# Linear attention followed by a gated MLP: in half of the batches the keys' sums become the stationary operand of the product with q

## The chip, the cores and the metric

The kernel runs on one core of a Trainium2 chip. Its engines work side by side: TensorE (PE in the profile; PEld is its loading of weights, the stationary operand), VectorE (DVE), ScalarE (ACT), GpSimd (POOL), and SyncE (SP), whose queue issues all DMAs here. PSUM is the memory that matmuls write; SBUF is where their operands lie. The metric is the device time of one execution in microseconds (us), as the median of several executions.

## What is computed

```python
# q, k, v: (8 batches, 8 heads, 576 positions, 64); omega: (128, 64); float32
def phi(x):                                   # x is scaled by 64 ** -0.25
    h = x @ omega.T - sum(x * x) / 2
    return exp(h - max(h)) / sqrt(128)        # 128 features of a position
q_p, k_p = phi(q), phi(k)
kv  = einsum('bhsm,bhsd->bhmd', k_p, v)       # 128 x 64 for a head
z   = sum(k_p, axis=2)                        # 128 for a head
num = einsum('bhsm,bhmd->bhsd', q_p, kv)
den = einsum('bhsm,bhm->bhs', q_p, z) + 1e-6
x   = (num / den) as 4608 rows of 512         # 8 heads x 64
out = (silu(x @ w_gate) * (x @ w_val)) @ w_out   # 512 -> 1536 -> 512
```

The MLP's weights come as 64-bit floats and are turned into 32-bit ones on the chip.

## The kernel before

**Groups and steps.** The attention is cut into groups of 256 positions of one pair of heads (`kgroups` and `qgroups`, L101 to L103). 576 positions give two such groups and 64 left over, and the left-over 64 positions of all four pairs make one more group, the one whose `gr` is None. So a batch has 9 groups of k and 9 of q. A step (L110 to L113) handles two groups: in steps 0 to 5 two of k, then 60 times one of q and one of k that lies 12 groups ahead, and in the last 6 steps two of q. A group of q goes through stages that are steps apart: projection and exponential (`st_transpose`, `st_project`, `st_max`, `st_exp`) in its own step, `q_transpose` one step later, `q_mult` two and `q_out` three steps later (L69 to L71).

**A group of q.** `st_exp` leaves the features `ph`: 128 positions on the partitions, 2 chunks by 2 heads by 128 features. `q_transpose` (L473) turns them by four PE transposes into `ptq` in PSUM, and ACT copies that to `qt`: 128 features on the partitions, 2 heads by 256 positions. `q_mult` (L486) has `qt` stationary: per chunk and head a matmul with 128 positions as columns of the weights, and `kvst`, 64 columns of kv and one of z, streams through. `po` then holds positions on the partitions, with the numerator in 64 columns and the denominator in the 65th. DVE adds the epsilon, inverts, and multiplies (L504 to L512) into `xn`. `q_out` (L520) turns `xn` by two transposes into `xt`, whose partitions are the 2 x 64 values of the two heads; ACT rounds it into `xh` and DVE takes the rest as `xl`, the MLP's x in two parts.

In the left-over group the four pairs have 64 positions each, so the weights are 64 columns wide, and two pairs use the two column halves of the array.

**The keys.** `k_accumulate` (L440) sums kv and z of two pairs in one PSUM tile `kvacc`, and `kv_finalize` (L433) copies it by ACT to `kvr` when all groups have been added, twice in a batch. z is the 65th column of `kvr`: a column of 128 features for each head.

**PSUM.** The tiles made by `ps_att` (L87) share one buffer of one bank: `pt` (the transposed inputs), `ptq`, `po` and `xt` follow one another in it. `pp`, `kvacc` and the MLP have buffers of their own.

**The MLP.** `stream` (L600) goes over ten tiles of up to 512 rows in rounds of two or three tiles, and over four sets of three weight slices in each round. A product is made of three matmuls of rounded parts: high by high, high by low, low by high. ACT makes the high part of a weight (`whi`, L237) and POOL the low part (`wlo`, L238); of the hidden layer, ACT makes `hh` (L641) and POOL `hl` (L642). `acc` collects a tile's rows over the sets, in buffers of the pool `accp`, which `om2` uses too.

**Order.** `ORDER` (L671) lists the nine stages of a step; after each of them `give` hands out a share of the step's MLP matmuls, so that attention and MLP are interleaved by a course that is worked out beforehand (L177 to L192). The framework may move an instruction ahead of one whose operands it reckons to be late; each engine then runs its own list strictly in order. Behind the loop the rest of the MLP runs alone.

Of the kernel before, what the change touches and what calls it, by code (L numbers as in the profile page):

```python
# [11 lines left out]
F32 = mybir.dt.float32  # L12
# [4 lines left out]
ALU = mybir.AluOpType  # L17
AX = mybir.AxisListType
# [5 lines left out]
def kernel(  # L24
# [11 lines left out]
    nc = tc.nc  # L36
    B, H, S, D = q.shape
    M = omega.shape[0]
    NT, DM = out.shape
    DF = w_gate.shape[1]  # L40
    P = 128
    NPAIR = H // 2
# [3 lines left out]
    NF = DF // P  # L46
    G = 256
    CH = G // P
# [6 lines left out]
    EPS = 1e-6 * M  # L55
    RES = S % G
# [8 lines left out]
    LAV = 1  # L65
    KLAG = 2
    TLAG = 1
    MLAG = 2
    OLAG = 3  # L69


    const = ctx.enter_context(tc.tile_pool(name="const", bufs=1))
    xres = ctx.enter_context(tc.tile_pool(name="xres", bufs=NXB))
    wpool = ctx.enter_context(tc.tile_pool(name="wpool", bufs=FA))
    moe = ctx.enter_context(tc.tile_pool(name="moe", bufs=2))
    accp = ctx.enter_context(tc.tile_pool(name="accp", bufs=11))
    dram = ctx.enter_context(tc.tile_pool(name="dram", bufs=1, space=DRAM))
    ps_m = ctx.enter_context(tc.tile_pool(name="ps_m", bufs=4, space=PSUM))
    att = ctx.enter_context(tc.tile_pool(name="att", bufs=2))
# [4 lines left out]
    ident = const.tile([P, P], F32, name="ident")  # L84
    make_identity(nc, ident)

    def ps_att(name, shape):  # L87
        return ps_a.tile(shape, F32, name=name, tag="b")
# [27 lines left out]
    def slots(n, kind):  # L116

        if not 0 <= n < NS:
            return []
        return [(i, b, g, (kgroups if kd == "k" else qgroups)[g]) for i, (kd, b, g) in enumerate(steps[n]) if kd == kind]  # L120

    def pairs_of(gr):
        return [(2 * c, 2 * c + 1) for c in range(CH)] if gr is None else [gr[:1]] * CH
# [3 lines left out]
    def column(b, gr):  # L127
        return b * S + (S - RES if gr is None else gr[1])
# [10 lines left out]
    def tile_of(col):  # L139
        j = max(j for j, (c, _) in enumerate(TILES) if c <= col)  # L140
        return j, col - TILES[j][0]
# [27 lines left out]
    for n in range(NS):  # L169
        for i, b, g, gr in slots(n, "q"):  # L170
            first = column(b, gr)
            for j in {tile_of(first)[0], tile_of(first + (RES if gr is None else G) - 1)[0]}:
                whole[j] = n + OLAG
                begun.setdefault(j, n + OLAG)


    NN = NS + OLAG + 1  # L177
    upper, lower = np.zeros(NN + 1), np.zeros(NN + 1)
# [48 lines left out]
    weights = {}  # L227
    converted = set()
# [48 lines left out]
    def tick():  # L277
        ticks[0] += 1
        next(wa, None)
# [74 lines left out]
    box = {}  # L354
# [3 lines left out]
    def st_transpose(n):  # L358
        if n >= NS:
            return  # L360
        nat = nats.pop(n)
        pt = (ps_moe if n < DENSE else ps_att)(f"pt_{n}", [P, 2, G])
        for i in range(2):
            for c in range(CH):
                nc.tensor.transpose(  # L365
                    pt[:, i, c * P : (c + 1) * P], nat[:, i, c].rearrange("p h d -> p (h d)"), ident
                )
        x = att.tile([P, 2, G], F32, name=f"x_{n}", tag="x")

        st = att.tile([P, 4, 2, CH, 2], F32, name=f"st_{n}", tag="st", bufs=6)  # L370
        sq = att.tile([P, 2, CH, 2, D], F32, name=f"sq_{n}", tag="sq")
        nc.gpsimd.tensor_tensor(sq, nat, nat, op=ALU.mult)  # L372
        nc.scalar.copy(x, pt)
        sts[n] = x, st, sq
        return True
# [51 lines left out]
    kvst = {}  # L427
# [5 lines left out]
    def kv_finalize(b, a2):  # L433
        acc = kvacc.pop((b, a2))
        raw = att.tile([P, 4, VW], F32, name=f"kvr{b}_{a2}", tag="kvr", bufs=4)
        nc.scalar.copy(raw, acc)
        for j in range(2):
            kvst[b, 2 * a2 + j] = raw[:, 2 * j : 2 * j + 2, :]

    def k_accumulate(n, half):  # L440

# [28 lines left out]
    qts = {}  # L470
    xns = {}

    def q_transpose(n):  # L473
        m = n
        n -= TLAG
        for _, b, g, gr in slots(n, "q"):
            ph = box.pop(("q", b, g))
            pt = (ps_moe if m < EARLY else ps_att)(f"ptq{b}_{g}", [P, 2, G])
            for hh in range(2):
                for c in range(CH):  # L480
                    nc.tensor.transpose(pt[:, hh, c * P : (c + 1) * P], ph[:, c, hh * M : (hh + 1) * M], ident)  # L481
            qts[b, g] = att.tile([P, 2, G], F32, name=f"qt{b}_{g}", tag="qt")
            nc.scalar.copy(qts[b, g], pt)
        return bool(slots(n, "q"))

    def q_mult(n):  # L486

        n -= MLAG
        for _, b, g, gr in slots(n, "q"):
            qt = qts.pop((b, g))  # L490
            po = ps_att(f"po{b}_{g}", [P, CH, 2, VW])
            for c in range(CH):
                prs = pairs_of(gr)[c]
                w = P // len(prs) if gr is None else P
                for j, pr in enumerate(prs if gr is None else prs[:1]):
                    for hh in range(2):
                        nc.tensor.matmul(  # L497
                            po[j * w : (j + 1) * w, c, hh, :],
                            qt[:, hh, c * P + j * w : c * P + (j + 1) * w],
                            kvst[b, pr][:, hh, :],  # L500
                            start=True, stop=True, skip_group_check=True,
                        )
            dn = att.tile([P, 2, CH, 2], F32, name=f"dn{b}_{g}", tag="dn", bufs=4)
            nc.vector.tensor_scalar_add(dn[:, 0], po[:, :, :, D], EPS)  # L504
            nc.vector.reciprocal(dn[:, 1], dn[:, 0])
            xn = att.tile([P, CH, 2, D], F32, name=f"xn{b}_{g}", tag="xn", bufs=3)
            nc.vector.tensor_tensor(
                xn.rearrange("p c h d -> p (c h) d"),
                po[:, :, :, 0:D].rearrange("p c h d -> p (c h) d"),
                dn[:, 1].rearrange("p c (h o) -> p (c h) o", o=1).broadcast_to([P, 2 * CH, D]),  # L510
                op=ALU.mult,
            )  # L512
            xns[b, g] = xn
        return bool(slots(n, "q"))
# [5 lines left out]
    def q_out(n):  # L520
        n -= OLAG
        for _, b, g, gr in slots(n, "q"):
            xn = xns.pop((b, g))
            po = ps_att(f"xt{b}_{g}", [P, G])
            first = column(b, gr)
            for c in range(CH):
                nc.tensor.transpose(po[:, c * P : (c + 1) * P], xn[:, c].rearrange("p h d -> p (h d)"), ident)  # L527
            j, o = tile_of(first)
            if gr is None:
                parts_ = [(po.rearrange("d (r c) -> d r c", c=RES), slice(0, NPAIR), j, o, RES)]  # L530
            else:
                cut = min(TILES[j][1] - o, G)
                parts_ = [(po[:, 0:cut], gr[0], j, o, cut)]
                if cut < G:
                    parts_.append((po[:, cut:G], gr[0], j + 1, 0, G - cut))
            for src, pr, j, o, w in parts_:
                if j not in xt:

                    while j - NXB >= 0 and not finished(j - NXB):
                        assert give(1), "the MLP waits for x, and x for the MLP"  # L540
                    xt[j] = [xres.tile([P, NPAIR, T], F32R, name=f"x{e}{j}", tag=f"x{e}") for e in "hl"]
                hi, lo = (t[:, pr, o : o + w] for t in xt[j])
                nc.scalar.copy(hi, src)
                nc.vector.tensor_tensor(lo, src, hi.bitcast(F32), op=ALU.subtract)  # L544
            if gr is None or gr[0] == NPAIR - 1:
                cols_done[0] = first + (RES if gr is None else G)
        return bool(slots(n, "q"))
# [23 lines left out]
    def finished(j):  # L571

        return at_visit[0] > last_visit[j]
# [83 lines left out]
    def give(us):  # L657
        debt[0] += us
        while debt[0] > 0:
            u = next(ma, None)  # L660
            if u is None:
                debt[0] = 0.0
                return False
            debt[0] -= u
            given[0] += u
        return True
# [3 lines left out]

    ORDER = (  # L671
        st_project,
        q_out,
        lambda n: st_transpose(n + 1),
        q_mult,
        lambda n: k_accumulate(n, 0),
        st_max,
        q_transpose,
        lambda n: k_accumulate(n, 1),
        st_exp,  # L680
    )

    for n in range(2):
# [7 lines left out]
    for n in range(NN):  # L691
        load(n + LA)
        load_v(n + LAV)
        want = OPS * np.interp(clock[n + 1], [clock[m] for m, _ in marks], [x for _, x in marks])
        for i, what in enumerate(ORDER):
            left = len(ORDER) - i
            what(n)
            due = course[n + 1] - given[0] - debt[0]
            if due > 0:
                give(due / left)  # L700
            for _ in range(int(np.ceil((want - ticks[0]) / left))):
                tick()
    for _ in ma:
        pass

# [29 lines left out]
```

## Time and profile before

| | |
|---|---|
| median of 3 runs | 1291.54 us (1289.42 to 1296.39) |
| profiled execution | 1285.57 us |
| its span, first to last instruction | 1283.8 us |
| granted TensorE clock, mean | 0.982 |
| matmul instructions | 7329 |
| DMA | 95.71 MB, 74 GB/s of HBM traffic over the span |

The span lies 1.8 us inside the time of its execution. Busy times of PE overlap: a matmul's duration in the profile is the time from its start until its result is out, and the next one starts long before. What a matmul costs is read from the distance between starts. A float32 matmul appears as two instructions (two passes), an fp32r matmul and a transpose as one.

### The profile page before, as it was taken

To read this page: it belongs to the slowest core of one execution; us is meant where nothing else is said; L and a number is where in the kernel's file an instruction comes from. 1 tells how busy PE (TensorE), PEld (TensorE's weight loads), DVE (VectorE), ACT (ScalarE), POOL (GpSimd) and SP (SyncE) were. 2 spreads that over 40 slices of the span, in tenths; PEclk is the share of its full clock that TensorE was granted. 3 is DMA by queue.
4 is the path that set the end of the run, shared out by engine and by line. 5 is a ranking of instruction groups with operands and counts; after the bars stand their busy time and mean duration, and the time that the engine had idled before them with its cause. 6 is when DMAs were issued, how large, how long until landed. Compare 5 with 4: busy or idle time off the path is not lost.

```text
span 1283.8 us, 19309 instructions
## 1 busy us (share of the span) xinstructions
PE 1243.3 (97%) x7329; PEld 1039.1 (81%) x7329; DVE 514.2 (40%) x1080; ACT 629.0 (49%) x1358; POOL 419.1 (33%) x364
## 2 busy tenths in 40 slices
PE   6988999999989999999999999999999999999998
PEld 5977778887868888888878888888888878888887
DVE  4787774457742343223333333223333321121212
ACT  4865666565344554555556653854544323222211
POOL 3454241545444121333333311433322113242421
PEclk7997899999989999999999999999999999999999
DMA  6557552345432122221222221211110111111112
GB/s 161 137 159 192 141 160 63 86 136 154 125 95 62 42 67 63 60 64 50 65 59 50 65 51 41 66 50 50 51 41 26 34 33 34 41 43 32 50 27 57
DMA packets 156477, 95.71 MB, mean 75 GB/s; under 512 B 119520, under 2 KB 131808, under 8 KB 156384
## 3 DMA queue, kind: packets, MB, share of 16 engines
q1 hardware_dynamic: 156384, 94.47, 28.0%
q8 instruction: 58, 0.95, 0.3%
q14 instruction: 35, 0.29, 0.1%
HBM read 75.56 MB, written 18.87 MB: 74 GB/s over the span
## 4 chain that ended last, share of the span: by engine, by line
PE 81%; DVE 7%; ACT 3%; issue 3%; POOL 2%; DMA 2%; SPq 1%; POOLq 0%; ACTq 0%; DVEq 0%
PE o L567 21%; PE g L558 21%; PE v L558 19%; PE pp L388 6%; PE kvacc L458 5%; PE po L497 4%; PE ptq L481 2%; PE pt L365 2%; ACT ph L420 1%; PE xt L527 1%; DVE st L261 1%; DVE st L406 1%; POOL wlo L238 1%; DMA nat<-in_k_dram 1%; SPq L323 1%
## 5 line engine op out<-in xcount | busy, mean ns | idle before, releaser
L642 POOL TENSOR_TENSOR hl<-sl,hh 128x512 fp32r<-128x512 f32 (+1 forms) x120 | 145.0, 1208 | 288.9 <-ACT hh L641 285.6
L238 POOL TENSOR_TENSOR wlo<-wraw,whi 128x512 fp32r<-128x512 f32 x108 | 138.9, 1299 | 251.7 <-ACT whi L237 230.0
L420 ACT ACTIVATE ph<-pp,st 128x128 f32<-128x128 f32 x576 | 166.6, 388 | 55.1 <-DVE st L409 54.0
L558 PE MATMUL g<-xh,whi 128*128 128x512 f32 (+1 forms) x480 | 184.4, 387 | 0.5 <-DVE sl L638 0.4
L558 PE MATMUL v<-xh,whi 128*128 128x512 f32 (+1 forms) x480 | 184.0, 383 | 0.0
L567 PE MATMUL o<-whi,hh 128*128 128x512 f32 x432 | 178.1, 412 | 2.4 <-ACT whi L237 1.7
L558 PE MATMUL g<-xl,whi 128*128 128x512 f32 (+1 forms) x480 | 180.0, 375 | 0.0
L558 PE MATMUL g<-xh,wlo 128*128 128x512 f32 (+1 forms) x480 | 178.8, 372 | 0.0
L558 PE MATMUL v<-xh,wlo 128*128 128x512 f32 (+1 forms) x480 | 178.1, 371 | 0.0
L558 PE MATMUL v<-xl,whi 128*128 128x512 f32 (+1 forms) x480 | 177.6, 370 | 0.0
L567 PE MATMUL o<-wlo,hh 128*128 128x512 f32 x432 | 171.5, 397 | 2.0 <-DVE st L408 1.4
L567 PE MATMUL o<-whi,hl 128*128 128x512 f32 x432 | 171.2, 396 | 0.3 <-POOL hl L642 0.2
L641 ACT CAST hh<-sl 128x512 fp32r<-128x512 f32 (+1 forms) x120 | 69.9, 584 | 172.7 <-DVE sl L638 172.3
L638 DVE TENSOR_TENSOR sl<-v,sl 128x512 f32<-128x512 f32 (+1 forms) x120 | 76.3, 636 | 188.0 <-PE v L558 181.9
L372 POOL TENSOR_TENSOR sq<-nat 128x512 f32<-128x512 f32 x72 | 77.4, 1076 | 213.0 <-DMA nat<-in_k_dram 192.8
L591 DVE TENSOR_TENSOR acc<-o,acc 128x512 f32<-128x512 f32 x108 | 74.3, 690 | 178.4 <-PE o L567 177.9
L406 DVE TENSOR_REDUCE st<-pp 128x4 f32<-128x512 f32 x144 | 93.5, 684 | 103.0 <-PE pp L388 103.0
L237 ACT CAST whi<-wraw 128x512 fp32r<-128x512 f32 x108 | 66.9, 623 | 103.9 <-PE v L558 58.5
L558 PEld LDWEIGHTS g<-xh,wlo 128*128 128x128 f32 x480 | 91.3, 190 | 15.2
L558 PEld LDWEIGHTS g<-xh,whi 128*128 128x128 f32 x480 | 91.2, 191 | 15.3 <-DVE sl L638 0.6
L558 PEld LDWEIGHTS v<-xh,wlo 128*128 128x128 f32 x480 | 90.4, 188 | 15.3
L558 PEld LDWEIGHTS g<-xl,whi 128*128 128x128 f32 x480 | 91.6, 191 | 13.2 <-DVE xl L544 0.3
(56 smaller groups left out, 1872.1 us busy)
## 6 DMA issues: line engine op xcount, KB each, us to landing
wraw<-wscr SPq DMA_DIRECT2D x108, 256.0 KB, 2.8
wscr<-wc SPq DMA_DIRECT2D x36, 256.0 KB, 2.2
out_dram<-acc SPq DMA_DIRECT2D x72, 128.0 KB, 2.3
nat<-in_k_dram SPq DMA_DIRECT2D x64, 128.0 KB, 3.1
v<-in_v_dram SPq DMA_DIRECT2D x64, 128.0 KB, 3.1
nat<-in_q_dram SPq DMA_DIRECT2D x64, 128.0 KB, 2.7
st<-in_moe_w_gate_dram SPq DMA_DIRECT2D x12, 512.0 KB, 4.4
st<-in_moe_w_val_dram SPq DMA_DIRECT2D x12, 512.0 KB, 4.6
```

The lines of the kernel that those rows point to most:

```text
L237: nc.scalar.copy(hi, raw)
L238: nc.gpsimd.tensor_tensor(lo, raw, hi.bitcast(F32), op=ALU.subtract)
L372: nc.gpsimd.tensor_tensor(sq, nat, nat, op=ALU.mult)
L388: nc.tensor.matmul(pp[hh][:, i, c, :], x[r, i, c * P : (c + 1) * P], omT[r], start=True, stop=True)
L406: nc.vector.tensor_reduce(st[:, 1, :, :, hh], pp[hh], axis=AX.X, op=ALU.max, negate=True)
L420: nc.scalar.activation(ph[:, c, hh * M : (hh + 1) * M], pp[hh][:, i, c, :], AF.Exp, bias=st[:, 3, i, c, hh : hh + 1], scale=1.0,)
L558: nc.tensor.matmul(ps, a_[:, ws], b_[:, c, :], start=n == 0, stop=n == 3 * NC - 1)
L567: nc.tensor.matmul(ps, a_[:, ts_], b_, start=first and n == 0, stop=last and n == 2)
L591: nc.vector.tensor_tensor(a_, po, a_, op=ALU.add)
L638: nc.vector.tensor_tensor(h, pv, h, op=ALU.mult)
L641: nc.scalar.copy(hh, h)
L642: nc.gpsimd.tensor_tensor(hl, h, hh.bitcast(F32), op=ALU.subtract)
```

## The change

For the batches 4 to 7 (`BPOOL = 4`, counted from 0) the product with q is turned round, and the division by the denominator is done ahead of it.

- `kv_finalize` also transposes the z columns of the two pairs (128 x 4) on PE into `zp` (4 x 128, in the shared PSUM buffer), copies them by ACT, and writes these 2 KB to DRAM.
- `load_z`, at the end of the step that has a batch's first group of q, reads them back with each row spread over all 128 partitions: two DMAs into `zt`, in a buffer of the raw weights that is no longer needed.
- `q_den`, a new last stage, one step behind the exponential: POOL multiplies `ph` by z (128 x 512; four instructions in the left-over group), DVE sums over the features, adds the epsilon and inverts.
- `q_norm`, a new second stage, two steps behind: POOL multiplies `ph` in place by these factors.
- `q_transpose` comes two steps behind the exponential in place of one, on the scaled `ph`.
- `q_mult` does nothing for these batches.
- `q_out` computes `xt` directly: for each head one matmul with 64 columns of `kvst` stationary and 256 columns of `qt` streaming, written to the head's half of the partitions (four pairs by 64 columns in the left-over group).

The pool `accp` has 10 buffers in place of 11, and `xn` shares two buffers with POOL's product, in place of three of its own. The batches 0 to 3 keep the old form.

```diff
-    accp = ctx.enter_context(tc.tile_pool(name="accp", bufs=11))
+    accp = ctx.enter_context(tc.tile_pool(name="accp", bufs=10))
...
+        if b >= BPOOL:
+            zp = ps_att(f"zp{b}_{a2}", [4, P])
+            nc.tensor.transpose(zp, raw[:, :, D], ident)
+            zs = att.tile([4, P], F32, name=f"zs{b}_{a2}", tag="zs")
+            nc.scalar.copy(zs, zp)
+            zd = dram.tile([4, P], F32, name=f"zd{b}_{a2}", tag="zd", bufs=4)
+            nc.sync.dma_start(zd, zs)
+            zds[b, a2] = zd
...
+    def load_z(n):
+        for _, b, g, gr in slots(n, "q"):
+            if g == 0 and b >= BPOOL:
...
+                zt = att.tile([P, 2, 4, M], F32, name=f"zt{b}", tag="stw")
+                for a2 in range(2):
+                    nc.sync.dma_start(
+                        zt[:, a2], zds.pop((b, a2)).rearrange("(o h) m -> o h m", o=1).broadcast_to([P, 4, M])
+                    )
+                    zbc[b, a2] = zt[:, a2]
...
+    def q_den(n):
+        n -= JLAG
...
+                nc.gpsimd.tensor_tensor(
+                    jk, ph, zt.rearrange("p (o h) m -> p o h m", o=1).broadcast_to([P, CH, 2, M]), op=ALU.mult
+                )
+            dn = att.tile([P, 3, CH, 2], F32, name=f"dj{b}_{g}", tag="dj", bufs=6)
+            nc.vector.tensor_reduce(dn[:, 0], jk, axis=AX.X, op=ALU.add)
+            nc.vector.tensor_scalar_add(dn[:, 1], dn[:, 0], EPS)
+            nc.vector.reciprocal(dn[:, 2], dn[:, 1])
+            dns[b, g] = dn
+
+    def q_norm(n):
+        n -= NLAG
...
+            nc.gpsimd.tensor_tensor(
+                phv, phv,
+                dn[:, 2].rearrange("p c (h o) -> p (c h) o", o=1).broadcast_to([P, 2 * CH, M]),
+                op=ALU.mult,
+            )
...
     def q_transpose(n):
         m = n
-        n -= TLAG
-        for _, b, g, gr in slots(n, "q"):
+        todo = [(b, g) for _, b, g, gr in slots(n - TLAG, "q") if b < BPOOL]
+        todo += [(b, g) for _, b, g, gr in slots(n - NLAG, "q") if b >= BPOOL]
+        for b, g in todo:
...
     def q_mult(n):
...
+            if b >= BPOOL:
+                continue
...
     def q_out(n):
...
+            if b < BPOOL:
+                xn = xns.pop((b, g))
+                for c in range(CH):
+                    nc.tensor.transpose(po[:, c * P : (c + 1) * P], xn[:, c].rearrange("p h d -> p (h d)"), ident)
+            else:
+                qt = qts.pop((b, g))
+                segs = [(pr, pr * RES, RES) for pr in range(NPAIR)] if gr is None else [(gr[0], 0, G)]
+                for pr, o, w in segs:
+                    for hh in range(2):
+                        nc.tensor.matmul(
+                            po[hh * D : (hh + 1) * D, o : o + w], kvst[b, pr][:, hh, 0:D], qt[:, hh, o : o + w],
+                            start=True, stop=True, skip_group_check=True,
+                        )
...
     ORDER = (
         st_project,
+        q_norm,
         q_out,
...
         st_exp,
+        q_den,
     )
```

More of the change, by code (lines that the diff above doesn't have):

```diff
@@ L67 @@
     TLAG = 1
+    JLAG = 1
+    NLAG = 2
     MLAG = 2
     OLAG = 3
+    BPOOL = 4
     const = ctx.enter_context(tc.tile_pool(name="const", bufs=1))
@@ L438, in kv_finalize @@
             kvst[b, 2 * a2 + j] = raw[:, 2 * j : 2 * j + 2, :]
+        if b >= BPOOL:
[6 more added lines that the diff above has]
+            zds[b, a2] = zd
+    zds = {}
+    zbc = {}
+    def load_z(n):
+        for _, b, g, gr in slots(n, "q"):
+            if g == 0 and b >= BPOOL:
+                assert len(converted) == 3 * NF, "the raw weights' buffers are still needed"
+                zt = att.tile([P, 2, 4, M], F32, name=f"zt{b}", tag="stw")
[4 more added lines that the diff above has]
+                    zbc[b, a2] = zt[:, a2]
@@ new lines @@
+    dns = {}
+    def q_den(n):
+        n -= JLAG
+        for _, b, g, gr in slots(n, "q"):
+            if b < BPOOL:
+                continue
+            ph = box["q", b, g].rearrange("p c (h m) -> p c h m", m=M)
+            jk = att.tile([P, CH, 2, M], F32, name=f"jk{b}_{g}", tag="jx")
+            if gr is None:
+                for c in range(CH):
+                    for j, pr in enumerate(pairs_of(gr)[c]):
+                        rows = slice(j * RES, (j + 1) * RES)
+                        zt = zbc[b, pr // 2][rows, 2 * (pr % 2) : 2 * (pr % 2) + 2, :]
+                        nc.gpsimd.tensor_tensor(jk[rows, c], ph[rows, c], zt, op=ALU.mult)
+            else:
+                pr = gr[0]
+                zt = zbc[b, pr // 2][:, 2 * (pr % 2) : 2 * (pr % 2) + 2, :]
+                nc.gpsimd.tensor_tensor(
[6 more added lines that the diff above has]
+            dns[b, g] = dn
@@ L440, in k_accumulate @@
+    def q_norm(n):
+        n -= NLAG
+        for _, b, g, gr in slots(n, "q"):
+            if b < BPOOL:
+                continue
+            dn = dns.pop((b, g))
+            phv = box["q", b, g].rearrange("p c (h m) -> p (c h) m", m=M)
+            nc.gpsimd.tensor_tensor(
[3 more added lines that the diff above has]
+            )
     def k_accumulate(n, half):
@@ L483, in q_transpose @@
             nc.scalar.copy(qts[b, g], pt)
-        return bool(slots(n, "q"))
     def q_mult(n):
@@ L489, in q_mult @@
         for _, b, g, gr in slots(n, "q"):
+            if b >= BPOOL:
+                continue
             qt = qts.pop((b, g))
@@ L505, in q_mult @@
             nc.vector.reciprocal(dn[:, 1], dn[:, 0])
-            xn = att.tile([P, CH, 2, D], F32, name=f"xn{b}_{g}", tag="xn", bufs=3)
+            xn = att.tile([P, CH, 2, D], F32, name=f"xn{b}_{g}", tag="jx")
             nc.vector.tensor_tensor(
@@ L522, in q_out @@
         for _, b, g, gr in slots(n, "q"):
-            xn = xns.pop((b, g))
             po = ps_att(f"xt{b}_{g}", [P, G])
             first = column(b, gr)
-            for c in range(CH):
-                nc.tensor.transpose(po[:, c * P : (c + 1) * P], xn[:, c].rearrange("p h d -> p (h d)"), ident)
+            if b < BPOOL:
+                xn = xns.pop((b, g))
+                for c in range(CH):
+                    nc.tensor.transpose(po[:, c * P : (c + 1) * P], xn[:, c].rearrange("p h d -> p (h d)"), ident)
+            else:
+                qt = qts.pop((b, g))
[6 more added lines that the diff above has]
+                        )
             j, o = tile_of(first)
@@ L702 @@
                 tick()
+        load_z(n)
     for _ in ma:
```

## The prediction, written before the result was known

> **What bounds the kernel now.** First the page: the share of each engine, and the chain that ended last.
>
> ```profile
> PE 1243.3 (97%) x7329; PEld 1039.1 (81%) x7329; DVE 514.2 (40%) x1080; ACT 629.0 (49%) x1358; POOL 419.1 (33%) x364
> ...
> PE 81%; DVE 7%; ACT 3%; issue 3%; POOL 2%; DMA 2%; SPq 1%; POOLq 0%; ACTq 0%; DVEq 0%
> ```
>
> PE is the bound. Is it so where the change acts? The `po` blocks of batch 3 end near 517 us and those of batch 7 near 1050 us (rows further down), so I cut the span there; the view gives each engine's busy time in a stretch.
>
> ```profile
> core 0: us, PE busy (x) PEld busy (x) DVE busy (x) ACT busy (x) POOL busy (x), PEclk, DMA share, GB/s
> ...
> 533.00:1060.00 527.00, 524.82 (x2995) 428.73 (x2995) 170.66 (x384) 278.22 (x554) 153.29 (x125) 1.00 0.20 51
> ```
>
> In the middle stretch PE is idle for 2.2 of 527 us, at full clock (1.00); POOL works 29% of it, DVE 32%. Behind it lies a fixed amount of MLP. So here a microsecond of PE work saved ends the kernel a microsecond earlier, and work of POOL or DVE costs nothing until PE waits for it.
>
> **What a block costs.** Durations of matmuls overlap, so a block's price is the distance between starts: from the MLP matmul ahead of it to the second one behind it, less two ordinary steps. The timeline of PE alone, at four places of the span:
>
> ```profile
> 787.00 0.39 PE L558 MATMUL v<-xh,whi 128*128 128x512 f32 x1
> 787.23 0.39 PE L558 MATMUL v<-xl,whi 128*128 128x512 f32 x1
> 787.45 0.39 PE L558 MATMUL v<-xh,wlo 128*128 128x512 f32 x1
> 787.68 0.38 PE L527 MATMUL xt<-ident,xn 128*128 128x128 f32 x2
> 787.82 0.48 PE L567 MATMUL o<-whi,hh 128*128 128x512 f32 x1
> 788.13 0.40 PE L567 MATMUL o<-wlo,hh 128*128 128x512 f32 x1
> ```
>
> ```profile
> 774.48 0.40 PE L567 MATMUL o<-whi,hh 128*128 128x512 f32 x1
> 774.71 1.02 PE L497 MATMUL po<-kvr,qt 128*128 128x65 f32 x8
> 775.55 0.47 PE L567 MATMUL o<-wlo,hh 128*128 128x512 f32 x1
> 775.86 0.39 PE L567 MATMUL o<-whi,hl 128*128 128x512 f32 x1
> ```
>
> ```profile
> 516.17 0.40 PE L567 MATMUL o<-whi,hh 128*128 128x512 f32 x1
> 516.50 0.73 PE L497 MATMUL po<-kvr,qt 128*64 128x65 f32 x16
> 517.16 0.50 PE L567 MATMUL o<-wlo,hh 128*128 128x512 f32 x1
> 517.50 0.39 PE L567 MATMUL o<-whi,hl 128*128 128x512 f32 x1
> ```
>
> ```profile
> 783.41 0.39 PE L558 MATMUL v<-xh,wlo 128*128 128x512 f32 x1
> 783.73 1.16 PE L388 MATMUL pp<-omT,x 64*128 64x128 f32 x16
> 784.82 0.50 PE L558 MATMUL v<-xh,whi 128*128 128x512 f32 x1
> 785.16 0.39 PE L558 MATMUL v<-xl,whi 128*128 128x512 f32 x1
> ```
>
> An ordinary step is 787.00 to 787.23, 0.23 us. Two transposes into `xt` cost 788.13 - 787.45 - 0.46 = 0.22. The eight passes of `po` cost 1.38 - 0.46 = 0.92, the sixteen passes with 64 columns of weights (left-over group) 1.33 - 0.46 = 0.87, the sixteen of the projection, with 64 rows, 1.75 - 0.46 = 1.29.
>
> How long does a float32 pass stream? Minimum durations of one line's matmuls:
>
> ```profile
> L388 PE MATMUL pp<-omT,x x1152: 271/272/579, 7.8 to 1000.4; 64*128 64x128 f32 x192
> ```
>
> ```profile
> L497 PE MATMUL po<-kvr,qt x640: 217/275/368, 48.2 to 1049.4; 128*128 128x65 f32 x128, 128*64 128x65 f32 x32
> ```
>
> 63 more columns take 271 - 217 = 54 ns more: 0.86 ns a column. So 65 columns stream 56 ns, 128 columns 110, and the new 256 columns 0.22 us.
>
> The sixteen half-width passes one after another would be 16 x 0.056 = 0.90 us, but from the first start to the MLP's next start are 0.66. So the two column halves ran side by side: 8 x 0.056 = 0.45, and 0.42 for entering and leaving this shape of the array. The projection agrees: 1.29 - 8 x 0.11 = 0.41. An `xt` or `po` block at full width shows little of this toll.
>
> **The change part by part.**
>
> Pair groups, 8 in a batch, 32 in all. Removed: `po` 0.92 and `xt` transposes 0.22, 1.14 us. Added: two matmuls of two passes, 64 columns of weights each, in opposite halves: 0.41 + 2 x 0.22 = 0.85. Saved 0.29 x 32 = 9.3 us.
>
> Left-over groups, 4: eight matmuls of 64 columns, sixteen passes as before, 0.87 both ways; the two transposes go, 0.22 x 4 = 0.9 us.
>
> The z transposes, 8. No row shows weights of 4 columns. By operation the nearest is a transpose at full width, 0.22 / 2 = 0.11; by shape it is a narrow block, toll 0.41 and 0.11, so 0.52. I take the narrow one, 4.2 us in all; the ends are 0.9 and 7.4, the latter if PE also waits each time for the copy of `kvr` (ACT copy of 0.39, row below).
>
> Waits of PE. `po` is one of the tenants of the shared PSUM bank, and its turn disappears:
>
> ```profile
> engine line waited for: us in total, times, longest us
> ...
> PEld po L497 <- ACT x L373: 5.8, 20, 0.6
> PEld pt L365 <- DVE xl L544: 3.7, 7, 0.9
> ...
> PE o L567 <- POOL hl L642: 0.2, 1, 0.2
> ```
>
> In the middle stretch these 5.8 us can go wholly, or the next tenant inherits them; half, 2.9, with 0 and 5.8 as ends. `zp` takes eight turns of its own.
>
> Work beside PE, costed at nothing while PE has its list full:
>
> ```profile
> L238 POOL TENSOR_TENSOR wlo<-wraw,whi 128x512 fp32r<-128x512 f32 x108 | 138.9, 1299 | 251.7 <-ACT whi L237 230.0 <-PE pt L365 17.9 <-PE o L567 2.2
> ...
> L399 DVE TENSOR_REDUCE st<-sq 128x8 f32<-128x512 f32 x72 | 49.2, 683 | 90.5 <-POOL sq L372 90.4
> ...
> L507 DVE TENSOR_TENSOR xn<-po,dn 128x256 f32<-128x256 f32 x72 | 30.4, 422 | 2.0
> ...
> L436 ACT COPY kvr<-kvacc 128x260 f32<-128x260 f32 x16 | 6.3, 392 | 7.7 <-PE kvacc L458 7.5
> ```
>
> POOL gets two products of 128x512 for a group; by `wlo` 1.30 each, 36 x 2.6 = 94 us, which raises it from 153 to 247 of 527 us. DVE swaps 0.42 for 0.68, 9 us more. The new way from `q_den` to `q_transpose` is 1.30 + 0.68 + 1.30 and two tiny DVE operations, about 3.6 us. `q_den` is the last stage of a step and `q_transpose` the ninth of eleven in the next; a step is 774.71 to the next `po` at
>
> ```profile
> 792.05 1.00 PE L497 MATMUL po<-kvr,qt 128*128 128x65 f32 x8
> ```
>
> 17 us, so there are about 12 us for it. What stands behind the two products on POOL is `wlo`, `hl` and `sq`. For `hl`, POOL's timeline and then PE's:
>
> ```profile
> 822.30 1.29 POOL L642 TENSOR_TENSOR hl<-sl,hh 128x512 fp32r<-128x512 f32 x1
> ```
>
> ```profile
> 834.44 0.39 PE L567 MATMUL o<-whi,hl 128*128 128x512 f32 x1
> ```
>
> It is used 10.9 us after it ends; 2.6 us of delay fit in. DMA: eight spreads of 256 KB and eight of 2 KB, on SP's queue. The page has the landing of a weight slice of that size, 2.8 us, and the waits of the queue have it standing still for up to 19.8 us at a time:
>
> ```profile
> wraw<-wscr SPq DMA_DIRECT2D x108, 256.0 KB, 2.8
> ```
>
> ```profile
> SPq L289 <- POOL wlo L238: 168.6, 48, 19.8
> ```
>
> A spread has one step, 17 us, until its first use. At worst it is 19.8 + 2.8 - 17 = 5.6 us late, four times, 22 us. I take nothing, since the weights that block the queue are fetched ahead of need. The accumulators: no round needs more than 10 buffers at once (2 + 4 + 4), so the eleventh costs nothing.
>
> Sum: 9.3 + 0.9 - 4.2 + 2.9 = 8.9 us. From 1285.57 us of the profiled execution to 1276.7, a factor of 0.9931. The runs shown have a median 0.5% above that execution; on 1291.54 the factor gives **1282.6 us**.
>
> **The rivals.**
>
> *The halves overlap only in part.* If matmuls start in the order of the program, the first head's second pass must end its turn before the other head begins: three passes in a row, 0.41 + 0.66 = 1.07. Then 32 x 0.07 = 2.2 in place of 9.3, net 1.8 us, 1289.7. In the sixteen-pass block the code issues four passes of one half, then four of the other; in strict order at least 13 turns of 0.056 = 0.73 us would show, and 0.66 are there. The Trainium skill, "TensorE: Matmul & The Clock Gate", Part 3, has matmuls start and end strictly in program order, which would be this rival; the 0.66 us do not agree with it.
>
> *They don't overlap*, say because streaming 256 columns twice at once is more than 65: 0.41 + 0.88 = 1.29, a loss of 0.15 x 32 = 4.8; net -5.2, 1296.8.
>
> *The narrow blocks eat the gain*: z at 7.4, no waits won: 9.3 + 0.9 - 7.4 = 2.8, 1288.7.
>
> *POOL's list holds PE: slower.* POOL runs in order and stands before `hl` for long (POOL's waits in the middle stretch, then the page's groups):
>
> ```profile
> POOL hl L642 <- ACT hh L641: 115.0, 29, 23.5
> ```
>
> ```profile
> L641 ACT CAST hh<-sl 128x512 fp32r<-128x512 f32 (+1 forms) x120 | 69.9, 584 | 172.7 <-DVE sl L638 172.3
> L638 DVE TENSOR_TENSOR sl<-v,sl 128x512 f32<-128x512 f32 (+1 forms) x120 | 76.3, 636 | 188.0 <-PE v L558 181.9
> ```
>
> If a group's scaling stands behind an `hl` that waits for PE's product, and the transposes come soon after that product on PE, PE stops for 0.64 + 0.58 (L638, L641) + 1.29 (`hl`) + 1.30 (scaling), 3.8 us at most. It decides from three late groups on (8.9 / 3.8); a third of 36 would be 46 us, net -37, about 1329. Against it: the 12 us of room, and that PE waits for POOL's `hl` only 0.2 us there today.
>
> **How the numbers follow.** Forecast 60%; partial overlap 10%; none 7%; gain eaten 10%; POOL holds PE 13%. 0.5%, 6.5 us, is about what a measurement of this kernel tells from no change. The forecast's own span: z at 0.9 and all waits won give 15.1 us, z at 7.4 with half the waits 5.7; four fifths of its chance lie beyond 6.5. So faster 0.48 + 0.02 from the eaten gain; same 0.12 + 0.10 + 0.04 + 0.08; slower 0.13 + 0.03. The range: 15.1 us gained give 1276, and the runs' lowest lies 2 us under their median, so 1274; no overlap with z at 7.4 gives 1300. It leaves out POOL's case and little else.
>
> **What would show it.** Right: the 128x64 block with 4 passes of 256 columns takes about 0.5 us from its first start to the MLP's next but for the toll, 0.85 by the same count; `po` ends near 517 us; PE idle in the middle stays at some 2 us; POOL at 45 to 50%. Wrong: 1.07 or 1.29 for that block, PE waiting for `ph` from POOL at `ptq`, or `zp` blocks far over 0.5 us.

## The result, and the profile after

The changed kernel takes 1277.64 us (median of 13 executions, 1273.21 to 1289.68), the kernel before 1288.56 us (13 executions, 1283.88 to 1296.39): a ratio of 0.9917, 95% interval 0.9893 to 0.9942. It is faster by 0.8%; the forecast was a factor of 0.9931, or 1282.6 us, with a range of 1274 to 1300. The profiled execution took 1277.26 us, 8.3 us less than that of before, its span is 1275.5 us and its granted clock 0.978 (0.982 before).

The page's shares of the engines and its chain, then the same middle stretch as before (us, then busy time and instructions of PE, PEld, DVE, ACT and POOL, clock, DMA share, GB/s):

```profile
PE 1233.1 (97%) x7137; PEld 1012.2 (79%) x7137; DVE 529.3 (41%) x1080; ACT 625.3 (49%) x1362; POOL 507.1 (40%) x448
...
PE 65%; DVE 2%; POOL 2%; issue 1%; ACT 1%; DMA 1%; SPq 0%; POOLq 0%; ACTq 0%
```

```profile
533.00:1060.00 527.00, 519.90 (x2843) 406.12 (x2842) 181.46 (x376) 276.87 (x562) 235.98 (x204) 1.00 0.21 54
```

The chain after covers only some 72% of the span, so its shares are not compared with those of before. POOL went from 153 to 236 us, 45% of the stretch, and DVE from 171 to 181. The clock is full here in both kernels. PE's idle time rose from 2.2 to 7.1 us. So PE was given less work, and part of the gain went into a new idle time. Two questions follow: what does a block cost now, and what does PE wait for?

**The blocks.** PE's timeline around the product that replaces `po` and the transposes, and around a `zp`:

```profile
638.67 0.39 PE L640 MATMUL v<-xh,wlo 128*128 128x512 f32 x1
638.98 0.65 PE L606 MATMUL xt<-qt,kvr 128*64 128x256 f32 x4
639.57 0.50 PE L640 MATMUL v<-xh,whi 128*128 128x512 f32 x1
639.90 0.39 PE L640 MATMUL v<-xl,whi 128*128 128x512 f32 x1
```

```profile
550.91 0.40 PE L640 MATMUL g<-xh,wlo 128*128 128x512 f32 x1
551.14 0.27 PE L446 MATMUL zp<-ident,kvr 128*4 128x128 f32 x1
551.17 0.47 PE L640 MATMUL g<-xh,whi 128*128 128x512 f32 x1
551.49 0.39 PE L640 MATMUL g<-xl,whi 128*128 128x512 f32 x1
```

By the same count as in the prediction (start ahead of the block to the second start behind it, less two steps of 0.23) the new block costs 639.90 - 638.67 - 0.46 = 0.77 us, and the median of all such blocks that stand alone is 0.78. Behind the x4 of the row lie four passes, whose records start at 638.98, 638.99, 639.25 and 639.26 us: two at a time, side by side. `zp` costs 0.58 - 0.46 = 0.12: weights of four columns show none of the toll that weights of 64 columns show.

**The waits.** In the window 520 to 1050 us (total us, times, longest), the weight loads and PE of the changed kernel, then PE of the kernel before:

```profile
PEld pt L369 <- DVE xl L626: 9.0, 9, 2.4
```

```profile
PE pt L369 <- DVE xl L626: 5.5, 6, 2.0
```

```profile
PE pt L365 <- DVE xl L544: 0.6, 2, 0.4
...
PE po L497 <- ACT x L373: 0.2, 1, 0.2
```

`pt`, the transpose of the next inputs, shares its PSUM bank with `xt`, and `xt` is free when DVE has made `xl` of it. This wait grew from 0.6 to 5.5 us of PE's time, which is the new idle time. The last row shows something else: the 5.8 us for which the weight loads of `po` waited before were only 0.2 us of PE.

One of these waits, on the timelines of ACT, DVE and POOL and then PE (start, duration; in brackets the idle time ahead and what ended it):

```profile
639.84 1.91 ACT L424 ACTIVATE ph<-pp,st 128x128 f32<-128x128 f32 x7 [4.17 <-DVE st L413]
641.60 0.41 ACT L625 CAST xh<-xt 128x256 fp32r<-128x256 f32 x1
```

```profile
642.36 0.69 DVE L491 TENSOR_REDUCE dj<-jk 128x4 f32<-128x512 f32 x1 [2.01 <-POOL jk L487]
642.96 0.41 DVE L626 TENSOR_TENSOR xl<-xt,xh 128x256 fp32r<-128x256 f32 x1
643.29 0.61 DVE L492 TENSOR_SCALAR dj<-dj 128x4 f32<-128x4 f32 x1
```

```profile
641.05 1.27 POOL L487 TENSOR_TENSOR jk<-ph,zt 128x512 f32<-128x512 f32 x1 [1.33 <-ACT ph L424]
```

```profile
643.43 0.66 PE L369 MATMUL pt<-ident,nat 128*128 128x128 f32 x4 [1.97 <-DVE xl L626]
```

`xt` was complete at 639.6. ACT put its exponentials first, so `xh` came at 641.60. On DVE the denominators' sum (L491) stands ahead of `xl` and itself waits for POOL's product, so `xl` started at 642.96 although `xh` was there at 642.01. PE stood still for 1.97 us.

Two ledgers are used below. The *length* is the time from the 469th record of a matmul into `v` to the 1081st, about 528 to 1077 us in the changed kernel, with the same MLP work in every kernel; the *blocks* are the sum of the prices of all attention blocks within it. Idle time of PE in front of such a block is included, idle time in front of an MLP matmul is not. A few records may be missing, which can shift the ends by some tenths. Before: length 558.0, blocks 133.2. After: 549.2 and 123.9. That stretch gained 8.8 us; the whole profiled execution gained 8.3.

### The profile page after: what moved, and what is told of

It reads as the page before. It is cut to its first block, busy times and chain, and to the rows that moved or that the text cites. A ratio compares the mean times of both kernels' runs of the same rounds, so it can differ in the third digit from the quotient of the medians.

```text
span 1275.5 us, 19029 instructions
## 1 busy us (share of the span) xinstructions
PE 1233.1 (97%) x7137; PEld 1012.2 (79%) x7137; DVE 529.3 (41%) x1080; ACT 625.3 (49%) x1362; POOL 507.1 (40%) x448
## 4 chain that ended last, share of the span: by engine, by line
PE 65%; DVE 2%; POOL 2%; issue 1%; ACT 1%; DMA 1%; SPq 0%; POOLq 0%; ACTq 0%
PE o L649 19%; PE g L640 19%; PE v L640 17%; PE pp L392 3%; PE kvacc L527 2%; PE pt L369 2%; PE ptq L551 1%; PE xt L606 1%; POOL jk L487 1%; PE po L568 1%; ACT ph L424 1%; DVE st L410 1%; DVE dj L491 0%; POOL wlo L242 0%; DMA nat<-in_k_dram 0%
## 5 line engine op out<-in xcount | busy, mean ns | idle before, releaser
L640 PEld LDWEIGHTS v<-xh,whi 128*128 128x128 f32 x480 | 90.5, 189 | 17.6 <-issue 2.7
```

The costliest lines, as they stand in the source:

```text
L640: nc.tensor.matmul(ps, a_[:, ws], b_[:, c, :], start=n == 0, stop=n == 3 * NC - 1)
```

## The experiments

Ratios are to the kernel before, with 95% intervals.

**Do the two halves overlap?** The 64-column halves were replaced by two full-width matmuls, which cannot lie beside each other, and then by one of them.

```diff
-                for pr, o, w in segs:
+                for hh in range(2 if gr is not None else 0):
+                    nc.tensor.matmul(
+                        po, kvst[b, gr[0]].rearrange("p h d -> p (h d)")[:, 0:P], qt[:, hh], start=True, stop=True, skip_group_check=True
+                    )
+                for pr, o, w in segs if gr is None else ():
```

> In the pair groups of batches 4 to 7 the two matmuls of the new product have 128 neighbouring columns of the keys' sums as weights and write all 128 partitions, the second over the first, so their values are not the attention's; four passes of 256 columns one after another, without the toll of the narrow shape. Theory A: the block costs 4 x 0.22 + 0.06 = 0.94 us in place of 0.78, 32 x 0.16 = 5 us more than the changed kernel, ratio to before 0.996. Theory C (the gain comes from PE's list being ordered otherwise, from one PSUM tenant less and from shorter waits, not from the block's price): as the changed kernel, 0.992.

The second kernel has `range(1 ...)` in the added loop.

> As the run with two full-width matmuls, but only the first of the two (two passes of 256 columns), so half of the product is left out. Theory A: the block costs 2 x 0.22 + 0.06 = 0.50 us in place of 0.78, 32 x 0.28 = 9 us less than the changed kernel, ratio to before 0.985. Theory C: as the changed kernel, 0.992.

PE's timeline with two matmuls, then with one:

```profile
562.12 0.39 PE L653 MATMUL o<-whi,hl 128*128 128x512 f32 x1
562.35 1.02 PE L605 MATMUL xt<-qt,kvr 128*128 128x256 f32 x4
563.02 0.58 PE L653 MATMUL o<-whi,hh 128*128 128x512 f32 x1
563.44 0.40 PE L653 MATMUL o<-wlo,hh 128*128 128x512 f32 x1
```

```profile
559.66 0.39 PE L653 MATMUL o<-whi,hl 128*128 128x512 f32 x1
559.89 0.59 PE L605 MATMUL xt<-qt,kvr 128*128 128x256 f32 x2
560.13 0.59 PE L653 MATMUL o<-whi,hh 128*128 128x512 f32 x1
560.56 0.40 PE L653 MATMUL o<-wlo,hh 128*128 128x512 f32 x1
```

Two passes cost 0.90 - 0.46 = 0.44, four one after another 1.32 - 0.46 = 0.86: 0.21 to 0.22 a pass, 0.86 ns a column, and no toll at full width. The changed kernel's four passes cost 0.78 with the toll. One after another they would have cost 0.86 and the toll on top, so the halves do run side by side, as the starts of their records show too: the change bought 0.86 - 0.44 = 0.42 by the overlap and paid 0.78 - 0.44 = 0.34 of it for the narrow shape.

The totals missed the expectations. The two-matmul kernel's ratio is 1.0019 (0.9994 to 1.0044), the one-matmul kernel's 0.9891 (0.9842 to 0.9940). PE's waits in the two-matmul kernel, from 520 to 1050 us, show a part of why ("issue" is time for which the profile shows no releaser):

```profile
PE pt L369 <- DVE xl L630: 8.2, 9, 2.1
PE pt L369 <- issue: 2.9, 1, 2.9
```

Of the two-matmul kernel's 13.4 us more in blocks (137.3 against 123.9), 8.4 stand at `pt` and 3.8 at `xt`; the wait for `xl` is 2.7 of the 8.4, and the one pause of 2.9 us is another part. In the one-matmul kernel `xt` costs 9.2 us less, but `pt` 2.8 more, and the wait for `xl` is 6.7. So a change in a block's length changes the waits as well: the total cannot price a block, only its own rows can. Why the waits grew in both was not followed further. In both kernels the longest of them were also followed by a lower clock (last section).

**What do the denominators cost?** They are left out.

```diff
     def load_z(n):
+        return
...
     def q_den(n):
+        return
...
     def q_norm(n):
+        return
```

> Leaves out the z transposes, their DRAM round trip, POOL's two products and DVE's sum and inversion for batches 4 to 7, so x is not divided by the denominator there; the matmuls of the new product stay. Theory A (PE's list sets the time, and the work of POOL, DVE and DMA is covered): against the changed kernel only the z transposes go, 8 x 0.12 = 1 us, and at most the 5 us of PE waits that came with the change; ratio to the kernel before 0.987 to 0.991. Theory B (the new way through POOL and DVE holds PE): 8 us or more faster than the changed kernel, ratio 0.985 or less, and PE's idle time in the middle stretch falls by as much.

The waits from 520 to 1050 us, of the weight loads and then of PE (so in the fences of waits that follow, where nothing else is said):

```profile
PEld pt L369 <- DVE xl L629: 2.6, 7, 0.6
```

```profile
PE pt L369 <- DVE xl L629: 0.2, 1, 0.2
```

The ratio is 0.9860 (0.9836 to 0.9884), between the two forecasts. The blocks cost 116.3 us, 7.6 less than in the changed kernel, and the `zp` blocks are only 0.7 of that; `pt` makes up 5.5 (17.5 to 12.0). So the 83 us of POOL and 11 of DVE in the middle are not all free: through one wait they cost PE some 5 us.

**Where does this wait come from?** Five kernels change what stands ahead of `xl`. First, no share of the MLP is handed out behind `q_norm` and `q_den`, which gives the nine shares of before:

```diff
-        for i, what in enumerate(ORDER):
-            left = len(ORDER) - i
+        paid = [w for w in ORDER if w not in (q_norm, q_den)]
+        for what in ORDER:
             what(n)
+            if what not in paid:
+                continue
+            left = len(paid) - paid.index(what)
```

> As the changed kernel, but the two new stages get no share of MLP work behind them, so a step has nine shares as before, not eleven. Theory S (the changed kernel's extra PE waits, input transposes pt waiting for DVE's xl, come from the smaller share of MLP between q_out and the input transposes): the waits fall by half, 2 to 3 us, ratio to before 0.989 to 0.990. Theory D (they come from DVE's sum of POOL's product, which stands in DVE's list ahead of xl and itself waits for POOL): waits as in the changed kernel, ratio 0.992.

Its waits of the weight loads and of PE:

```profile
PEld pt L369 <- DVE xl L626: 5.2, 5, 1.9
```

```profile
PE pt L369 <- DVE xl L626: 3.0, 4, 1.5
```

0.9886 (0.9850 to 0.9922): the wait falls by half, but the interval reaches to the changed kernel's ratio. Nor is the wait all that changed: the blocks fall by 4.5 us, and in 11 places, not 2, projection and product now stand behind each other, which alone is worth 9 x 0.20 = 1.8 us (the price of such a meeting follows below). Second, `pt` itself comes later:

```diff
-        lambda n: st_transpose(n + 1),
         q_mult,
+        lambda n: st_transpose(n + 1),
```

> As the changed kernel, but the input transposes come behind q_mult's place, one stage later, so that the shared PSUM bank has another share of MLP work to come free in. If PE's waits for xl at that bank are what the change lost (5 us): ratio to before 0.988. If not, 0.992.

0.9939 (0.9909 to 0.9969). PE's wait falls to 1.9 us in the middle and the length there to 544.6, but the order holds for the batches 0 to 3 too, and there `po` now meets the same `xl`. PE's wait from 0 to 520 us:

```profile
PE po L568 <- DVE xl L626: 14.6, 10, 7.6
```

In the changed kernel PE waits there for `xl` 6.6 us at `pt` and 1.5 at `po`, so some 6.5 us are new. Third, DVE sums `ph` itself and does not wait for POOL's product:

```diff
-            nc.vector.tensor_reduce(dn[:, 0], jk, axis=AX.X, op=ALU.add)
+            nc.vector.tensor_reduce(dn[:, 0], ph, axis=AX.X, op=ALU.add)
```

> As the changed kernel, but DVE sums ph, not POOL's product of ph and z, so the denominators are other numbers; POOL's products, DVE's work and the DMAs stay in amount. Theory D (DVE waits for POOL with xl behind it): PE's waits for xl at the input transposes fall from 14 us to about the 3 us of the run without denominators, ratio 0.987. Theory L (DVE's additional load, or POOL's, is what delays xl): as the changed kernel, 0.992.

PE's wait:

```profile
PE pt L369 <- DVE xl L626: 2.8, 3, 1.5
```

The changed kernel's figure to set beside it is 5.5 (the 14 us of the expectation add the weight loads' 9.0, which overlap it). The ratio is 0.9904 (0.9881 to 0.9927), and the blocks fall by only 0.8 us. DVE's wait for POOL is half of the wait at `pt` at most, and most of what it gave was lost elsewhere: PE's wait at `o` for POOL's `hl`, for one, is 1.7 us against 0.6. Fourth, a rival: DVE's tiny addition of epsilon, which is long when POOL runs. The changed kernel's groups on DVE in the same window (count, busy us, mean ns, idle us before):

```profile
L492 DVE TENSOR_SCALAR dj<-dj 128x4 f32<-128x4 f32 x36 | 11.0, 306 | 0.5
L493 DVE RECIPROCAL dj<-dj 128x4 f32<-128x4 f32 x36 | 6.4, 176 | 1.1
```

```diff
-            nc.vector.tensor_scalar_add(dn[:, 1], dn[:, 0], EPS)
-            nc.vector.reciprocal(dn[:, 2], dn[:, 1])
+            nc.vector.reciprocal(dn[:, 2], dn[:, 0])
```

> The changed kernel without the addition of epsilon in the denominators of batches 4 to 7 (that part is left out): DVE inverts the sum as it stands. In the changed kernel this tiny DVE operation (128x4) takes 157 ns at least, 306 ns in the mean and 744 at most, and in the kernel with two widths its end at 581.25 us was that of a POOL product; the reciprocal behind it never takes longer than 180 ns. Theory P (DVE's addition is held by POOL's product, and the rest of x, xl, stands behind it on DVE, for which PE waits at pt): the waits of PE and its weight loads for xl in 520 to 1050 us, 5.5 and 9.0 us in the changed kernel, fall to 4 us in sum or less per view, and the ratio to the kernel before is about 0.988. Theory G (PE waits because of where q_out comes among ACT's exponentials and DVE's sum; the addition does not matter): the waits stay at 5 us and 8 us or more, and the ratio is 0.991 to 0.992.

Its waits of the weight loads and of PE:

```profile
PEld pt L369 <- DVE xl L625: 8.7, 9, 2.2
```

```profile
PE pt L369 <- DVE xl L625: 5.2, 6, 1.8
```

The ratio is 0.9920 (0.9894 to 0.9945): the same number of waits of nearly the same length. Theory P falls. The addition is held, but what is behind it had room. Fifth, the sum itself is put behind `xl`: it is made in `q_norm`, which now comes behind `q_out`, and a tiny copy of a column of `xl` holds it back. So POOL's scaling comes later too.

```diff
+            if lastlo[0] is not None:
+                nc.vector.tensor_copy(dn[:, 0, 0, 0:1], lastlo[0][:, 0:1].bitcast(F32))
+            nc.vector.tensor_reduce(dn[:, 0], jks.pop((b, g)), axis=AX.X, op=ALU.add)
...
-        q_norm,
-        q_out,
+        lambda n: None,
+        lambda n: (q_out(n), q_norm(n)),
```

> The changed kernel with DVE's part of the denominator (sum, epsilon, inverse) put behind the rest of x, xl, of the same step on DVE: a tiny copy of one column of xl into the tile that the sum writes holds the sum back. POOL's product stays where it is, and the shares of the MLP stay at their places. In the changed kernel, of 30 xl in the middle the four latest for DVE's sake start 1.2 to 1.9 us after xh, the high part that ACT makes, with the sum between them, and the mean from the end of xh to the start of xl is 0.44 us (0.05 without denominators). Theory S (the sum that waits for POOL's product stands ahead of xl): this mean falls to 0.1 us, the waits at pt for xl (9.0 us weight loads, 5.5 us PE) to 5 and 3 us or less, and the ratio to the kernel before is about 0.989. Theory A (it is ACT, whose exponentials stand ahead of xh): the waits stay at 7 and 4 us or more, and the ratio is about 0.992. A later scaling of the features by POOL may bring a wait at ptq; then the ratio is 0.992 or more with the waits at pt gone.

The weight loads' and then PE's waits from 520 to 1050 us:

```profile
PEld ptq L555 <- POOL ph L507: 7.4, 7, 1.8
...
PEld pt L369 <- DVE xl L630: 3.3, 7, 0.7
```

```profile
PE ptq L555 <- POOL ph L507: 4.4, 5, 1.4
...
PE pt L369 <- DVE xl L630: 0.5, 2, 0.3
```

The mean from the end of `xh` to the start of `xl`, over all groups whose `xt` starts from 533 to 1050 us, falls from 0.43 to 0.05 us, and the wait at `pt` from 5.5 to 0.5 us of PE. In its place PE waits 4.4 us at `ptq` for the features that POOL scales later, a wait that the changed kernel does not have at all. The ratio is 0.9915 (0.9883 to 0.9946): nothing gained. Theory S has the cause of the wait at `pt`, and the last sentence of the expectation has the total. Here the chain of product, sum and scaling costs PE about the same whether x or the features are late (5.5 us against 0.5 + 4.4).

**An order with room for both.** Now `q_norm` comes first, and `q_out` right behind the projection, with no MLP between them:

```diff
     ORDER = (
-        st_project,
         q_norm,
+        st_project,
         q_out,
...
+        paid = [w for w in ORDER if w not in (q_norm, q_den, st_project)]
```

> As the run with nine shares, but q_norm comes first in a step and nothing stands between st_project and q_out, so that projection and product run one behind the other more often. Both are narrow shapes of the array; the two places in the changed kernel where they are neighbours cost 1.87 us, against 1.29 + 0.78 apart, so a meeting saves 0.20. If the toll is paid for each change of shape: some 20 more meetings in batches 4 to 7, 4 us, and 1 us in the batches before, ratio 0.988. If the toll isn't shared in general: 0.992, or more, since xt and the projection's tiles then ask DVE and ACT at the same time.

PE's timeline of a meeting of the two blocks, and all of PE's waits from 520 to 1050 us:

```profile
560.23 0.39 PE L640 MATMUL g<-xh,wlo 128*128 128x512 f32 x1
560.55 1.16 PE L392 MATMUL pp<-omT,x 64*128 64x128 f32 x16
561.64 0.65 PE L606 MATMUL xt<-qt,kvr 128*64 128x256 f32 x4
562.22 0.50 PE L649 MATMUL o<-whi,hh 128*128 128x512 f32 x1
562.56 0.39 PE L649 MATMUL o<-wlo,hh 128*128 128x512 f32 x1
```

```profile
PE o L649 <- POOL hl L724: 1.8, 2, 1.1
PE po L568 <- ACT x L377: 0.8, 1, 0.8
```

1264.20 us, a ratio of 0.9812 (0.9789 to 0.9836): this order beats both kernels, and it computes all that the reference asks for. The waits for `xl` at `pt` and for POOL at `ptq` are both gone. `xt` now comes right behind the projection, and `xh` starts 0.12 us after it in the mean (0.33 in the changed kernel, where ACT's exponentials at times stand between them, as at 639.84 above). And the two blocks together cost 2.33 - 0.46 = 1.87 us; apart they cost 1.29 + 0.78 = 2.07. There are 27 such meetings in the stretch, against 2 in the changed kernel: 25 x 0.20 = 5.0 us, and `pt` costs 12.0 in place of 17.5. Blocks: 110.7 us, 13.2 less, of which these two make up 10.5; the other 2.7 are not assigned here. The length falls by 12.1, and the medians differ by 13.4.

The same closeness, without the change:

```diff
-            left = len(ORDER) - i
+            left = len(ORDER) - max(i, 1)
             what(n)
+            if i == 0:
+                continue
```

> The kernel before, with nothing put between st_project and q_out, as in the run that has them together. There xt is two transposes at full width, which cost 0.23 us alone and 0.17 behind the projection: about 15 more meetings in batches 4 to 7 and as many ahead save 30 x 0.06 = 2 us, ratio 0.998. If the gain of having them together came from elsewhere than the shared toll of two narrow shapes (the order of the lists, the waits at the PSUM bank), it would show here as well: 0.990 or less.

0.9930 (0.9905 to 0.9955), more than expected. A meeting of `pp` with the full-width `xt` of before saves only 0.06 (1.46 against 1.29 + 0.23), and before has 11 of them already, so 16 more give 1.0; the stretch gained 4.6 us in all, spread over several kinds of block, and the rest of the 8.7 us between the medians lies outside it, unexplained. So the change's own worth, at the closer order, is 0.9812 / 0.9930 = 0.988 (0.985 to 0.992, if the two intervals are independent).

And that order without the denominators, by the same edit as above:

> The run that has projection and product together, less the z transposes, the DRAM round trip, POOL's products and DVE's sums of batches 4 to 7, so x is not divided by the denominator there. In that run PE no longer waits for xl at the input transposes. Theory A (all of this work is then covered): 1 us for the z transposes, ratio as there less 0.001, 0.980. Theory B (POOL and DVE still hold PE elsewhere): 0.976 or less.

0.9785 (0.9745 to 0.9824), between the two. The blocks are 110.6 against 110.7 us: in this order POOL's and DVE's new work adds nothing ahead of PE's attention blocks. The length is 1.7 us shorter, nearly all of it between MLP matmuls; PE's wait at `o` for POOL's `hl` is 1.1 us against 1.8. Where the rest of the 3.5 us lies by which the ratios differ is not settled, and the two intervals overlap.

**The buffers.** The kernel before with `accp` at 10 and `xn` at 2 buffers:

```diff
-    accp = ctx.enter_context(tc.tile_pool(name="accp", bufs=11))
+    accp = ctx.enter_context(tc.tile_pool(name="accp", bufs=10))
...
-            xn = att.tile([P, CH, 2, D], F32, name=f"xn{b}_{g}", tag="xn", bufs=3)
+            xn = att.tile([P, CH, 2, D], F32, name=f"xn{b}_{g}", tag="xn", bufs=2)
```

> The kernel before with 10 accumulator buffers in place of 11 and two buffers of xn in place of three, nothing else. If these buffers are never all in use: 1.000. If they were: PE waits for acc or xn, 1.003 or more.

1.0006 (0.9982 to 1.0030), blocks 133.2 as before. The buffers cost nothing.

## Why the prediction was right, and where it was not

- **The bound.** PE at full clock bounded the stretch, and its saved work came out at the end, less the new idle time: right.
- **Pair groups.** The mechanism was right: the halves overlap, and the blocks' price decides. Size: 0.85 forecast, 0.78 measured. The toll, 0.41 by the projection and 0.42 by the left-over block, was 0.34 here. Saved 0.36 x 32 = 11.5 us in place of 9.3.
- **A reading that does not hold.** That a `po` block at full width shows little of the toll does not follow from the prediction's pass of 0.056 us: 0.92 - 8 x 0.056 leaves 0.47. In the trace the eight passes of the block at 774.71 start 0.11 us apart, and so do the loads of their weights: 8 x 0.11 = 0.88 of its 0.92. The prices of whole blocks, and so the sum, do not rest on that reading.
- **Left-over groups.** Forecast 0.87 for both forms; the new one is 0.82 (median), so 0.27 x 4 = 1.1 in place of 0.9.
- **The z transposes.** The row nearest by operation (0.11) was right, the row nearest by shape (0.52) was taken. Measured 0.12 x 8 = 1.0 in place of 4.2.
- **Waits of PE: the step that failed.** The forecast was a gain of 2.9 us; PE lost 5. Two errors lie in it. The 5.8 us belonged to PE's weight loads, which run ahead of the matmuls; PE itself waited 0.2 us there, so there was next to nothing to win. And the shared bank's other tenant got a new wait: the chain of product, sum and scaling was followed up to `ptq`, where it had room, but not what stands behind the sum on DVE. That is `xl`, and `pt` waits for it. The prediction listed what stands behind POOL's products and left DVE's queue out. So its sign that PE's idle time in the middle stays at some 2 us did not come: it is 7.1.
- **POOL's list holds PE.** POOL's share came as forecast, 45% of the stretch. The rival's place (`hl`, then the scaling, then `ptq`) did not show in the changed kernel: no wait at `ptq` for POOL. A relative of it did, through DVE, at about a tenth of its price (5 of 46 us); where the sum was held back, it showed at `ptq` itself, 4.4 us.
- **No cost for DMA and buffers:** no wait of PE or POOL for the landing of `zt` shows, and the buffers' run shows no cost.

Sum by measured terms: 11.5 + 1.1 - 1.0 - 5.0 = 6.6 us, against 8.3 between the profiled executions; 1.7 stay unassigned. The forecast was 8.9. That it came near is luck: three terms that were too cautious (by 2.2, 0.2 and 3.2 us) made up for most of one that had the wrong sign (7.9 us).

On the overlap, the Trainium skill, "TensorE: Matmul & The Clock Gate", Part 3, has matmuls start and end strictly in program order. The prediction's rival took this pass by pass, which would have made this block the partial overlap of 1.07 us; the measured 0.78 does not agree with that reading. Taken for whole matmuls of two passes, the rule is not contradicted by this block: the trace does not say which head a record belongs to, and two heads that take turns (638.98 and 639.25, 638.99 and 639.26 us) would start and end in order.

## What to carry to other kernels

Read a wait of weight loads beside PE's own row for the same tile: only the second is time to win. When an engine that is a third busy gets a new chain of work, list what stands behind each of its instructions on every engine that it passes, the middle one too; here it was DVE's sum, not POOL's products. If moving that instruction only hands the wait on, look for an order in which both consumers have room, and put blocks of narrow shape next to each other.

## What was not expected of the hardware

- **Two narrow blocks behind each other cost less than apart.** A projection and a 64-column product cost 1.87 us in place of 2.07, though their shapes differ. By the blocks the toll of the 64-column product alone is 0.34 us (0.78 against 0.44), so the 0.20 are a part of the two tolls, not a whole one. The Trainium skill, "TensorEngine Tiling (Array Packing)", section "Key Properties", says that a change of the tiling mode drains TensorE; whether the toll is this drain no run here shows. That weights of four columns pay none (0.12) no run here explains.
- **A tiny DVE operation is held while POOL works.** The addition of epsilon to 128x4 numbers takes 306 ns in the mean, the reciprocal of the same tile 176. In the kernel with two full-width matmuls:

```profile
579.95 1.28 POOL L728 TENSOR_TENSOR hl<-sl,hh 128x512 fp32r<-128x512 f32 x1 [0.26 <-ACT hh L727]
```

```profile
580.44 0.81 DVE L492 TENSOR_SCALAR dj<-dj 128x4 f32<-128x4 f32 x1
```

It ends at 581.25, 0.02 us after POOL's product. This is no single case: of the changed kernel's 36 additions 15 take longer than 0.2 us, and each of these ends 0.02 to 0.03 us behind an operation of POOL; the other 21 take 0.16 to 0.17. The reciprocal, 180 ns at most, is not held, though it too runs beside POOL. The Trainium skill, "SBUF — State Buffer", section "SBUF: two separate sides", has DVE and GpSimd share a pair of ports as an exclusive lock, held for a whole instruction, for DVE operations in a mode of two ports or with two inputs in SBUF. The ends of the additions agree with it; in which mode they run no run here shows. No effect on the time of this kernel shows in the run without the addition.
- **Behind a pause of over 2 us the clock was at half.** From 520 to 1080 us, the pauses of PE that were longer than 2 us are three, all at `pt`: 2.07 and 2.87 us in the kernel with two full-width matmuls, 2.52 in that with one. Behind each the clock fell; stretches of the first kernel and of the second:

```profile
950.00:955.00 5.00, 3.37 (x10) 2.90 (x11) 2.13 (x6) 1.51 (x4) 5.00 (x5) 0.66 0.16 52
```

```profile
643.00:648.00 5.00, 5.00 (x18) 4.09 (x17) 1.28 (x2) 0.62 (x1) 2.75 (x3) 0.66 0.23 54
```

The granted clock is 0.66 there, a stretch of 3.4 us at 0.5, in which MLP matmuls start 0.43 us apart in place of 0.23. No other kernel's clock falls between 520 and 1080 us; the changed kernel's longest pause there is 1.97. So a long wait cost more than itself; three cases do not show where the limit lies.
